# Attention and a mixture of experts on one core: sums of w2 pinned to other steps, a w1 load moved ahead, the last window in another sequence

## The chip, the cores and the metric

One Trainium2 chip, one core of it. The metric is the device time of one execution in microseconds (us). The engines are TensorE (PE in the profile), VectorE (DVE), ScalarE (ACT), GpSimd (POOL) and SyncE (SP), which here only issues DMAs. Each takes its own instructions in order.

## The reference

Attention over 4 x 8 heads of length 1152 and head size 64, where the queries are averaged in pairs; its result, reshaped, is x with 2304 tokens (N) of 512 features (D). Then a mixture of E = 8 experts with F = 1024 hidden units each, in float32:

```
logits = x @ w_gate
P = exp(logits - logits.max())
for _ in range(8):
    P /= P.sum(1, keepdims=True) + 1e-09
    P /= P.sum(0, keepdims=True) + 1e-09
    P *= N / E
for e in range(E):
    out += P[:, e:e+1] * (np.maximum(x @ w1[e], 0) @ w2[e])
```

The eight rounds are called the Sinkhorn here. Their sums over axis 0 go over all tokens, so over all partitions.

## The kernel before, in words

Every float32 product is made of three fp32r products of a high and a low part (hi x hi, lo x hi, hi x lo). "Cut" means making the two parts: hi by ScalarE (a copy to fp32r), lo by VectorE (the source less hi).

The work has three phases. The attention runs to about 371 us by a plan of its own. `moe()` (L825 to L1004) then takes the first of three groups of 768 tokens through all experts, to about 904.6 us. `late()` (L1016 on) takes groups 2 and 3, to the end at 1878.6 us.

`moe()` has 32 steps, k = (expert, quarter of F). A step makes seven products of a Strassen-like scheme for the hidden block (`product`, L886 to L894, weights of w1 stationary), combines them on VectorE (`plus`, L911), applies the relu and cuts the result (`hidden`, L900 and L901). The second products with w2 (`second`, L924; matmuls L921) are taken from a list three at a time (`some_second`) and added to x by VectorE (L937, L941). Within a step the code also prepares the next weights (class `Weights`):
- `sums1(k+1)` makes the four sums of w1's blocks that the scheme needs (L143 to L146), on VectorE for k from 2 to 8, else on GpSimd; they are the tile w1t.
- `cut1(k+1)` cuts the seven w1 blocks (w1h L157, w1l L162) and stores both parts to DRAM on SP (L170, w1c), so that `late()` need not make them again.
- `load1(k+2)` (L128) loads raw w1 (tile w1s), `cut2(k)` (L175, L176) cuts w2, `load2(k+1)` (L135) loads raw w2 into w2r or w2s in turn.
- `late()` wants four sums of each w2 block too (`sums2`, L182 to L185, on GpSimd). From step k = LATER = 5 on, `whole2(k)` makes them in place in the raw w2 tile and stores the block (w2c, L191, SP). For blocks 0 to 4 `half2` reloads one half of a block into a tile xt (L196), makes the sums and stores the half (L200); its ten calls stand in steps 10 to 19.
- The Sinkhorn on the gate matrix PR is a generator, `fill` (L855 to L880), advanced at four places of each step. Its sums over partitions are all-reduces on GpSimd: L860 (maximum) once, L875 eight times. VectorE reads their result at L862 and L876.
- In the last four steps `blocks.add` (L91 to L103) makes on GpSimd the differences of x that group 2's scheme needs.

The order of the instructions on each engine in `moe()` is made by a scheduler of the framework from what is ready. Only instructions handed to `keep_in_program_order` stay behind the ones that the code has before them on their engine: `cut2` and `blocks.add(1, ...)`. The sums and stores of w2 and the halves are not among them, and the scheduler is free to put them earlier.

`late()` is different: it hands operations with costs and priorities (`op`, smaller is earlier) to a `Plan` that lists them by engine under limits of buffers (`LATE_CAPS`), and the result stands as written. It has 64 steps (32 windows of two steps). `load_ops` (L1071) issues on SP, in order of priority: w1 of the window's first step (T - 21), the gate's row pb (T - 20), w2 (T - 16; raw parts L1087 and L1088, sums L1089), w1 of the second step (T - 7). `step_ops` makes the first products (L1064) from the stored w1 cuts; `window_ops` (L1189) makes the second products transposed (L1266): `hsum` (L1207, GpSimd) makes sums of hidden blocks hb, `cuts` the hi and lo parts of w2's and the hidden blocks (L1228 to L1243); ScalarE copies accumulators into PSUM ahead of a product where PRE or PRE_END names it (L1251), else VectorE adds the product to x (L1280). In the last window (`end`) EARLY sets how early the w2 cuts may be made and PRE_END which accumulators are fetched ahead. `join` (L1301) adds the accumulators of a group together; `finish` (L1320) transposes them (L1335), copies the result out of PSUM into tiles os, of which there are three (L1346, L1348), and stores half rows of tokens (L1353).

Of the kernel before, what the change touches and what calls it, by code (L numbers as in the profile page):

```python
# [5 lines left out]
F32 = mybir.dt.float32  # L6
# [105 lines left out]
LATER = 5  # L112


class Weights:
# [63 lines left out]
    def sums2(self, k, t):  # L179
        b11, b21, b12, b22 = t  # L180
        e = self.nc.gpsimd
        e.tensor_tensor(out=b22, in0=b12, in1=b22, op=ALU.add)  # L182
        e.tensor_tensor(out=b12, in0=b11, in1=b12, op=ALU.subtract)
        e.tensor_tensor(out=b11, in0=b22, in1=b11, op=ALU.subtract)
        e.tensor_tensor(out=b21, in0=b21, in1=b11, op=ALU.subtract)  # L185

    def whole2(self, k):
        t = self.raw2[k]
        self.sums2(k, [t[:, a, b * 2 * P:(b + 1) * 2 * P] for a in range(2) for b in range(2)])
        y = self.summed[k] = self.cuts.tile([P, 2 * D], F32, name=f"w2c{k}")  # L190
        self.nc.sync.dma_start(out=y.rearrange("p (a d) -> p a d", a=2), in_=t)  # L191

    def half2(self, k, h):
        t = self.stage.tile([P, 2, TH], F32, name="xt", tag="xt", bufs=2).rearrange("p a t -> p (a t)")[:, :4 * P].rearrange("p (a d) -> p a d", a=4)
        ds = slice(h * P, (h + 1) * P)
        self.nc.sync.dma_start(out=t, in_=self.w2[k].rearrange("p (a d) -> p a d", a=4)[:, :, ds])  # L196
        self.sums2(k, [t[:, a] for a in range(4)])
        if h == 0:
            self.summed[k] = self.cuts.tile([P, 2 * D], F32, name=f"w2c{k}")
        self.nc.sync.dma_start(out=self.summed[k].rearrange("p (a d) -> p a d", a=4)[:, :, ds], in_=t)  # L200
# [624 lines left out]
def moe(tc, out, x, ident, wg, PR, blocks, wt):  # L825
    nc = tc.nc
    with (
# [133 lines left out]

        for k in range(wt.steps):
# [15 lines left out]
            if k == 0:  # L978
                wt.cut2(0)
            wt.load1(k + 2)  # L980
            if k:
                wt.cut2(k)
            wt.load2(k + 1, "w2r" if k % 2 else "w2s")
            if k >= LATER:
                wt.whole2(k)
            if k >= wt.steps - 4:
                blocks.add(1, (3, 4, 6, 5)[k - wt.steps + 4], nc.gpsimd)
# [5 lines left out]
            if 10 <= k < 10 + 2 * LATER:  # L993
                wt.half2((k - 10) // 2, k % 2)
# [5 lines left out]
        for i in (0, 3, 4, 1, 5, 2, 6):  # L1000
            blocks.hi(1, i)
            blocks.lo(1, i)
        some_second(MT)
# [3 lines left out]
PRE, PRE_END = (0, 1, 2, 3, 4), (0, 2, 3)  # L1007
EARLY = 8
ORDER = (0, 0), (6, 2), (5, 5), (3, 3), (4, 4), (1, 1), (2, 6)
LATE_CAPS = dict(pb=2, w1=2, w2=2, hb=2, ht=1, hc=3, wc=3, e=2, mt=2, os=3)  # L1010
# [5 lines left out]
def late(tc, out, x, ident, blocks, wt):  # L1016
# [54 lines left out]
    def load_ops(j):  # L1071
        T = 28 * j
        g, e = 1 + j // PW, j % PW // 2
        if j % 2 == 0:
            @op("SP", 1600, T - 20, w=[("pb", g, e)], new=[(("pb", g, e), "pb")], lat=2500)
            def load_pb():
                y = D0["pb", g, e] = tile("pb", [TG])
# [13 lines left out]
        for s in range(2):  # L1091
            k = 2 * j + s

            @op("SP", 7000, T + 14 * s - 21, w=[("w1", k)], new=[(("w1", k), "w1")], lat=2500)
# [94 lines left out]
    def window_ops(j):  # L1189
# [10 lines left out]
        def hsum(i, a, b, r, prio):  # L1200
            new = [(HT, "ht")] if i == 5 else []

            @op("Pool", pool(2 * TH), prio, r=r, w=full({3: 3, 4: 2, 6: 1}[i]) if i != 5 else [HT], new=new, use=[HB])
# [231 lines left out]
```

## Time and profile before

| | |
|---|---|
| three executions, us | 1882.83, 1882.98, 1880.57; median 1882.83 |
| the profiled execution | 1880.4 us, of which the span from first to last instruction is 1878.6 |
| mean granted TensorE clock | 0.989 of full speed |
| busy, share of the span | TensorE 97%, VectorE 79%, ScalarE 61%, GpSimd 37% |
| the chain that ended last | TensorE 85%, VectorE 6%, GpSimd 3%, nothing the profile shows 2%, DMA 2%, ScalarE 1% |
| DMA | 366.88 MB in all, 195 GB/s mean |

Times within the profile are from the span's start. A timeline row gives start, duration, engine, line and operation, the output and input tiles, how many instructions it stands for, and in brackets how long the engine was idle before it and what released it ("issue": the engine waited for nothing that the profile shows). In the rows by stretch, busy time is given for each engine with the count of its instructions; PEclk is the mean TensorE clock that was granted, as a share of full speed. SPq is SyncE's queue of DMA issues.

### The profile page before, as it was taken

To read this page: it belongs to the slowest core of one execution; us is meant where nothing else is said; L and a number is where in the kernel's file an instruction comes from. 1 tells how busy PE (TensorE), PEld (TensorE's weight loads), DVE (VectorE), ACT (ScalarE), POOL (GpSimd) and SP (SyncE) were. 2 spreads that over 40 slices of the span, in tenths; PEclk is the share of its full clock that TensorE was granted. 3 is DMA by queue.
4 is the path that set the end of the run, shared out by engine and by line. 5 is a ranking of instruction groups with operands and counts; after the bars stand their busy time and mean duration, and the time that the engine had idled before them with its cause. 6 is when DMAs were issued, how large, how long until landed. Compare 5 with 4: busy or idle time off the path is not lost.

```text
span 1878.6 us, 32317 instructions
## 1 busy us (share of the span) xinstructions
PE 1826.6 (97%) x12324; PEld 1722.8 (92%) x12324; DVE 1481.7 (79%) x2653; ACT 1146.5 (61%) x1900; POOL 703.1 (37%) x533
## 2 busy tenths in 40 slices
PE   9999999989798999999899999999989999999997
PEld 8888888978687999998799999999989999999996
DVE  8999999788667777776468777777797878878776
ACT  7888887643223333333277677776766777777774
POOL 5555555421256434353223323233252323323224
PEclk9999999999999999999899999999999999999998
DMA  6787776386178666562754655556455565655541
GB/s 209 186 212 192 203 193 170 96 283 224 74 274 293 240 219 225 212 221 82 285 201 173 218 187 197 205 180 222 176 193 186 185 205 191 225 183 193 205 160 34
DMA packets 100279, 366.88 MB, mean 195 GB/s; under 512 B 15804, under 2 KB 39324, under 8 KB 91932
## 3 DMA queue, kind: packets, MB, share of 16 engines
q1 hardware_dynamic: 96668, 362.85, 57.6%
q8 instruction: 97, 1.59, 0.3%
q10 hardware_dynamic: 3456, 1.97, 0.3%
q14 instruction: 58, 0.48, 0.1%
HBM read 252.77 MB, written 80.34 MB: 177 GB/s over the span
## 4 chain that ended last, share of the span: by engine, by line
PE 85%; DVE 6%; POOL 3%; issue 2%; DMA 2%; ACT 1%; POOLq 0%; SPq 0%; DVEq 0%; ACTq 0%
PE mt L1266 23%; PE pso L921 10%; PE ps L566 7%; PE bA L1064 7%; PE bD L1064 7%; PE bB L1064 7%; PE ps L643 4%; PE ps L675 3%; PE bC L1064 3%; PE psh L891 3%; PE ps L689 3%; PE psh L893 3%; PE psh L892 3%; PE ps L694 1%; DVE c L911 1%
## 5 line engine op out<-in xcount | busy, mean ns | idle before, releaser
L1266 PE MATMUL mt<-hc,wc 128*128 128x384 f32 x2616 | 520.8, 335 | 5.9 <-DVE hc L1243 4.3
L1266 PEld LDWEIGHTS mt<-hc,wc 128*128 128x128 f32 x2616 | 457.7, 188 | 8.6 <-DVE hc L1243 5.9
L1207 POOL TENSOR_TENSOR hb<-hb 128x768 f32<-128x768 f32 x96 | 210.9, 2197 | 352.5 <-DVE hc L1243 347.8
L1233 DVE TENSOR_TENSOR wc<-w,wc 128x512 fp32r<-128x512 f32 x218 | 221.3, 1015 | 36.6 <-ACT wc L1228 36.6
L1243 DVE TENSOR_TENSOR hc<-hb,hc 128x768 fp32r<-128x768 f32 x192 | 190.1, 990 | 44.2 <-ACT hc L1238 44.1
L574 DVE TENSOR_SCALAR_CACHE_REDUCE E<-ps 128x384 f32<-128x384 f32 x432 | 214.9, 551 | 10.3 <-PE ps L566 9.2
L1238 ACT ACTIVATE hc<-hb 128x768 fp32r<-128x768 f32 x192 | 161.6, 842 | 51.4 <-DVE hb L1159 35.2
L1278 ACT ACTIVATE x<-mt 128x768 f32<-128x768 f32 x162 | 131.9, 814 | 99.9 <-PE mt L1266 99.5
L587 ACT ACTIVATE E<-E,st 128x1152 f32<-128x1152 f32 x144 | 179.9, 1261 | 16.8 <-DVE st L580 16.7
L1207 POOL TENSOR_TENSOR ht<-hb 128x768 f32<-128x768 f32 x32 | 60.8, 1899 | 317.0 <-DVE hb L1159 317.0
L891 PE MATMUL psh<-xch,w1h 128*128 128x384 f32 x448 | 154.3, 344 | 19.1 <-DVE u L911 5.4
L1064 PE MATMUL bA<-xch,w 128*128 128x384 f32 x512 | 151.3, 336 | 8.4 <-DMA w<-w1c 8.4
L893 PE MATMUL psh<-xch,w1l 128*128 128x384 f32 x448 | 153.3, 343 | 2.2 <-DVE w1l L162 2.2
L900 ACT ACTIVATE hh<-c 128x384 fp32r<-128x384 f32 x128 | 66.4, 522 | 145.4 <-DVE c L911 138.8
L892 PE MATMUL psh<-xcl,w1h 128*128 128x384 f32 x448 | 153.0, 341 | 0.0
L1064 PE MATMUL bD<-xch,w 128*128 128x384 f32 x512 | 151.3, 336 | 0.2 <-ACT bD L1122 0.2
L921 PE MATMUL pso<-w2h,hh 128*128 128x512 f32 x384 | 149.6, 391 | 1.8 <-DVE x L941 1.8
L1064 PE MATMUL bB<-xch,w 128*128 128x384 f32 x512 | 150.9, 335 | 0.0
L921 PE MATMUL pso<-w2l,hh 128*128 128x512 f32 x384 | 150.2, 391 | 0.0
L921 PE MATMUL pso<-w2h,hl 128*128 128x512 f32 x384 | 150.1, 391 | 0.0
L1228 ACT ACTIVATE wc<-w 128x512 fp32r<-128x512 f32 x218 | 135.9, 624 | 22.6 <-PE mt L1266 18.4
L566 PE MATMUL ps<-kT,qT 64*128 64x384 f32 (+1 forms) x1296 | 146.2, 346 | 0.1
(195 smaller groups left out, 3957.4 us busy)
## 6 DMA issues: line engine op xcount, KB each, us to landing
w<-w1c SPq DMA_DIRECT2D x64, 1792.0 KB
w<-w2c SPq DMA_DIRECT2D x64, 512.0 KB
F<-T SPq DMA_DIRECT2D x168, 184.0 KB
w1c<-w1h SPq DMA_DIRECT2D x32, 896.0 KB
w1c<-w1l SPq DMA_DIRECT2D x32, 896.0 KB
w1s<-in_moe_w_dram SPq DMA_DIRECT2D x32, 512.0 KB
w<-in_moe_w_dram SPq DMA_DIRECT2D x64, 256.0 KB
qr<-in_q_dram SPq DMA_DIRECT2D x15, 640.0 KB
```

The lines of the kernel that those rows point to most:

```text
L566: nc.tensor.matmul(ps[h][:, :PK], D["qT", p][rows, x, t * P:(t + 1) * P], D["kT", p][rows, y, j * PK:(j + 1) * PK], start=(i == 0), stop=( ...
L574: nc.vector.tensor_scalar(out=D["E", m, h][:, j * PK:(j + 1) * PK], in0=D["sc", m, j][h][:, :PK], scalar1=0.0625, scalar2=None, op0=ALU.mu ...
L587: nc.scalar.activation(out=x, in_=x, func=ACTF.Exp, bias=D["st", m][:, h, 3:4], accum_out=sums[p % RS][:, col + h * QT:col + h * QT + 1])
L891: nc.tensor.matmul(ps, hi[:, a, c, :], blocks.xch[:, b, c, :], start=(c == 0), stop=False)
L892: nc.tensor.matmul(ps, hi[:, a, c, :], blocks.xcl[:, b, c, :], start=False, stop=False)
L893: nc.tensor.matmul(ps, lo[:, a, c, :], blocks.xch[:, b, c, :], start=False, stop=(c == 1))
L921: nc.tensor.matmul(ps, u[:, fh, ms], w, start=(n == 0), stop=(n == 11))
L1064: nc.tensor.matmul(o, w, v, start=start, stop=stop, skip_group_check=True)
L1207: nc.gpsimd.tensor_tensor(out=hblock(i), in0=D0[HB][:, a], in1=D0[HB][:, b], op=sub)
L1233: nc.vector.tensor_tensor(out=y[:, 1], in0=wsrc(), in1=y[:, 0].bitcast(F32), op=sub)
L1243: nc.vector.tensor_tensor(out=y[:, 1], in0=hblock(b), in1=y[:, 0].bitcast(F32), op=sub)
L1266: nc.tensor.matmul(o, w[:, y, s, ds], v[:, z, s], start=(i == 0 and not pre), stop=(i == 5), skip_group_check=pre)
```

## The change

It touches four places.
- w2's sums: LATER is 9, so blocks 0 to 8 are reloaded in halves (18 instead of 10), and whole blocks are summed from k = 9. A half is now a job of three stages: load in step 9 + n, sums a step later, store a step after that. All sums, loads and stores of it, the sums of whole blocks, and their stores are pinned in program order. The store of block k - 1 stands in step k between the w1 load and the w2 load, and the last two are issued on ScalarE's queue after the cuts of group 2's x.
- The additions for group 2 at the last four steps stand ahead of the loads.
- `late()`: the first pb tile is allocated first, and w1 of the second step is loaded right behind w1 of the first.
- The end: EARLY, PRE_END, the last window's sums hsum on VectorE and ahead, its cuts in another sequence, and four tiles xs in place of os for the output's first three token tiles.

```diff
@@ -109,7 +109,7 @@
         self.nc.vector.tensor_tensor(out=self.xcl[:, i], in0=self.src(g, i), in1=self.xch[:, i].bitcast(F32), op=ALU.subtract)
-LATER = 5
+LATER = 9
 class Weights:
@@ -176,28 +176,32 @@
         self.tc.keep_in_program_order(self.nc.vector.tensor_tensor(out=lo, in0=self.raw2[k], in1=hi.bitcast(F32), op=ALU.subtract))
         self.b[k] = (hi, lo)
-    def sums2(self, k, t):
+    def sums2(self, t):
         b11, b21, b12, b22 = t
-        e = self.nc.gpsimd
-        e.tensor_tensor(out=b22, in0=b12, in1=b22, op=ALU.add)
-        e.tensor_tensor(out=b12, in0=b11, in1=b12, op=ALU.subtract)
-        e.tensor_tensor(out=b11, in0=b22, in1=b11, op=ALU.subtract)
-        e.tensor_tensor(out=b21, in0=b21, in1=b11, op=ALU.subtract)
+        e, pin = self.nc.gpsimd, self.tc.keep_in_program_order
+        pin(e.tensor_tensor(out=b22, in0=b12, in1=b22, op=ALU.add))
+        pin(e.tensor_tensor(out=b12, in0=b11, in1=b12, op=ALU.subtract))
+        pin(e.tensor_tensor(out=b11, in0=b22, in1=b11, op=ALU.subtract))
+        pin(e.tensor_tensor(out=b21, in0=b21, in1=b11, op=ALU.subtract))
     def whole2(self, k):
         t = self.raw2[k]
-        self.sums2(k, [t[:, a, b * 2 * P:(b + 1) * 2 * P] for a in range(2) for b in range(2)])
+        self.sums2([t[:, a, b * 2 * P:(b + 1) * 2 * P] for a in range(2) for b in range(2)])
+
+    def store2(self, k, q):
         y = self.summed[k] = self.cuts.tile([P, 2 * D], F32, name=f"w2c{k}")
-        self.nc.sync.dma_start(out=y.rearrange("p (a d) -> p a d", a=2), in_=t)
+        self.tc.keep_in_program_order(q.dma_start(out=y.rearrange("p (a d) -> p a d", a=2), in_=self.raw2[k]))
     def half2(self, k, h):
         t = self.stage.tile([P, 2, TH], F32, name="xt", tag="xt", bufs=2).rearrange("p a t -> p (a t)")[:, :4 * P].rearrange("p (a d) -> p a d", a=4)
         ds = slice(h * P, (h + 1) * P)
-        self.nc.sync.dma_start(out=t, in_=self.w2[k].rearrange("p (a d) -> p a d", a=4)[:, :, ds])
-        self.sums2(k, [t[:, a] for a in range(4)])
+        self.tc.keep_in_program_order(self.nc.sync.dma_start(out=t, in_=self.w2[k].rearrange("p (a d) -> p a d", a=4)[:, :, ds]))
+        yield
+        self.sums2([t[:, a] for a in range(4)])
         if h == 0:
             self.summed[k] = self.cuts.tile([P, 2 * D], F32, name=f"w2c{k}")
-        self.nc.sync.dma_start(out=self.summed[k].rearrange("p (a d) -> p a d", a=4)[:, :, ds], in_=t)
+        yield
+        self.tc.keep_in_program_order(self.nc.sync.dma_start(out=self.summed[k].rearrange("p (a d) -> p a d", a=4)[:, :, ds], in_=t))
 class Plan:
@@ -959,6 +963,7 @@
                 if todo:
                     second(*todo.pop(0))
+        jobs = []
         for k in range(wt.steps):
             hids[k] = [hid.tile([P, 2, TG], F32R, name=nm, tag=nm) for nm in ("hh", "hl")]
             p1 = keep(product(k, 0, 0), "p1")
@@ -977,21 +982,25 @@
             wt.cut1(k + 1)
             if k == 0:
                 wt.cut2(0)
+            if k >= wt.steps - 4:
+                blocks.add(1, (3, 4, 6, 5)[k - wt.steps + 4], nc.gpsimd)
             wt.load1(k + 2)
             if k:
                 wt.cut2(k)
+            if LATER < k < wt.steps - 1:
+                wt.store2(k - 1, nc.sync)
             wt.load2(k + 1, "w2r" if k % 2 else "w2s")
             if k >= LATER:
                 wt.whole2(k)
-            if k >= wt.steps - 4:
-                blocks.add(1, (3, 4, 6, 5)[k - wt.steps + 4], nc.gpsimd)
+            if 9 <= k < 9 + 2 * LATER:
+                jobs.append(wt.half2((k - 9) // 2, (k - 9) % 2))
+            for y in jobs:
+                next(y, None)
             if k == 0:
                 last_gate()
                 fill = sinkhorn()
             if k == 2 * FQ:
                 spread()
-            if 10 <= k < 10 + 2 * LATER:
-                wt.half2((k - 10) // 2, k % 2)
             some_second(3)
             next(fill, None)
             next(fill, None)
@@ -1000,14 +1009,16 @@
         for i in (0, 3, 4, 1, 5, 2, 6):
             blocks.hi(1, i)
             blocks.lo(1, i)
+        for k in (wt.steps - 2, wt.steps - 1):
+            wt.store2(k, nc.scalar)
         some_second(MT)
 SLOT = 1040
-PRE, PRE_END = (0, 1, 2, 3, 4), (0, 2, 3)
-EARLY = 8
+PRE, PRE_END = (0, 1, 2, 3, 4), (0, 1, 3, 4)
+EARLY = 12
 ORDER = (0, 0), (6, 2), (5, 5), (3, 3), (4, 4), (1, 1), (2, 6)
-LATE_CAPS = dict(pb=2, w1=2, w2=2, hb=2, ht=1, hc=3, wc=3, e=2, mt=2, os=3)
+LATE_CAPS = dict(pb=2, w1=2, w2=2, xs=4, hb=2, ht=1, hc=3, wc=3, e=2, mt=2, os=3)
 OUT = {(0, 0): 1, (0, 1): 6, (1, 0): 2, (1, 1): 3}
@@ -1074,7 +1085,7 @@
         if j % 2 == 0:
             @op("SP", 1600, T - 20, w=[("pb", g, e)], new=[(("pb", g, e), "pb")], lat=2500)
             def load_pb():
-                y = D0["pb", g, e] = tile("pb", [TG])
+                y = D0["pb", g, e] = tile("pb", [TG]) if j else first_pb
                 n = (g - 1) * MT
                 nc.sync.dma_start(out=y, in_=wt.spread[e, n:n + MT].rearrange("n t -> (n t)").unsqueeze(0).to_broadcast([P, TG]))
@@ -1091,7 +1102,7 @@
         for s in range(2):
             k = 2 * j + s
-            @op("SP", 7000, T + 14 * s - 21, w=[("w1", k)], new=[(("w1", k), "w1")], lat=2500)
+            @op("SP", 7000, T + 14 * s - (21 if k != 1 else 34.5), w=[("w1", k)], new=[(("w1", k), "w1")], lat=2500)
             def load_w1(k=k):
                 y = D0["w1", k] = tile("w1", [2, 7, 2, P], F32R)
                 nc.sync.dma_start(out=y.bitcast(F32), in_=wt.kept[k % (E * FQ)])
@@ -1200,11 +1211,11 @@
         def hsum(i, a, b, r, prio):
             new = [(HT, "ht")] if i == 5 else []
-            @op("Pool", pool(2 * TH), prio, r=r, w=full({3: 3, 4: 2, 6: 1}[i]) if i != 5 else [HT], new=new, use=[HB])
+            @op("DVE" if end else "Pool", dve(2 * TH) if end else pool(2 * TH), prio, r=r, w=full({3: 3, 4: 2, 6: 1}[i]) if i != 5 else [HT], new=new, use=[HB])
             def hsums():
                 if new:
                     D0[HT] = tile("ht", [2, TH])
-                nc.gpsimd.tensor_tensor(out=hblock(i), in0=D0[HB][:, a], in1=D0[HB][:, b], op=sub)
+                (nc.vector if end else nc.gpsimd).tensor_tensor(out=hblock(i), in0=D0[HB][:, a], in1=D0[HB][:, b], op=sub)
         def cuts(n, a, b):
             slot = T + 4 * n + 1
@@ -1279,19 +1290,33 @@
                     else:
                         nc.vector.tensor_tensor(out=y, in0=t, in1=y, op=ALU.add)
-        cuts(0, *ORDER[0])
-        cuts(1, *ORDER[1])
-        hsum(5, 2, 3, full(2) + full(3), T - 1)
-        cuts(2, *ORDER[2])
-        hsum(3, 3, 0, full(3) + full(0), T + 1)
-        cuts(3, *ORDER[3])
-        hsum(4, 2, 3, full(2) + full(3), T + 5)
-        cuts(4, *ORDER[4])
-        if j % PW == PW - 1:
+        if end:
+            cuts(0, *ORDER[0])
+            cuts(1, *ORDER[1])
+            hsum(5, 2, 3, full(2) + full(3), T - 1)
+            hsum(3, 3, 0, full(3) + full(0), T)
+            hsum(4, 2, 3, full(2) + full(3), T + 1)
+            cuts(2, *ORDER[4])
+            cuts(3, *ORDER[2])
+            cuts(4, *ORDER[3])
             join(g)
-        cuts(5, *ORDER[5])
-        hsum(6, 1, 2, full(1) + full(2), T + 14)
-        cuts(6, *ORDER[6])
+            cuts(5, *ORDER[5])
+            hsum(6, 1, 2, full(1) + full(2), T + 14)
+            cuts(6, *ORDER[6])
+        else:
+            cuts(0, *ORDER[0])
+            cuts(1, *ORDER[1])
+            hsum(5, 2, 3, full(2) + full(3), T - 1)
+            cuts(2, *ORDER[2])
+            hsum(3, 3, 0, full(3) + full(0), T + 1)
+            cuts(3, *ORDER[3])
+            hsum(4, 2, 3, full(2) + full(3), T + 5)
+            cuts(4, *ORDER[4])
+            if j % PW == PW - 1:
+                join(g)
+            cuts(5, *ORDER[5])
+            hsum(6, 1, 2, full(1) + full(2), T + 14)
+            cuts(6, *ORDER[6])
         if end:
             finish(g)
@@ -1316,6 +1341,9 @@
         both(4, 4, 3, T + 5)
         both(3, 5, 3, T + 6)
         both(6, 4, 6, T + 7)
+
+    def late_tile():
+        return sb.tile([P, 2, TH], F32, name="xs", tag="xs", bufs=4).rearrange("p a t -> p (a t)")[:, :D]
     def finish(g):
         T = 28 * PW * g + 27
@@ -1334,13 +1362,13 @@
                     for db in range(2):
                         nc.tensor.transpose(y[:, (2 * dh + db) * P:(2 * dh + db + 1) * P], acc(g, OUT[dh, th])[:, db, ts], ident)
-                nos = [] if dh else [(OS, "os")]
+                nos = [] if dh else [(OS, "os" if i > 2 else "xs")]
                 @op(("ACT", "DVE"), [act(256), dve(256)], pr + dh * (1.5 if th else 3) + 0.5, r=[("t", g, i, dh), own[i]] + ([("o", g, i, 0)] if dh else []),
                     w=[("o", g, i, dh)], new=nos, use=[OS] if dh else [])
                 def put(eng, i=i, dh=dh, OT=OT, OS=OS):
                     if dh == 0:
-                        D0[OS] = tile("os", [D])
+                        D0[OS] = tile("os", [D]) if i > 2 else late_tile()
                     y, z = (t[:, dh * 256:dh * 256 + 256] for t in (D0[OS], D0[OT]))
                     if eng == "ACT":
                         nc.scalar.activation(out=y, in_=z, func=ACTF.Copy)
@@ -1371,6 +1399,7 @@
             def x_lo(i=i):
                 blocks.lo(g, i)
+    first_pb = tile("pb", [TG])
     seed("B")
     seed("C")
     for g in range(1, G):
```

## Rows read from the trace of the kernel before

**Rows 1.** Busy time by stretch: each engine's us (instructions), then PEclk, DMA share, GB/s.

```profile
371.00:420.00 49.00, 43.52 (x235) 39.12 (x233) 40.18 (x89) 22.18 (x40) 15.13 (x25) 0.97 0.78 275
480.00:499.00 19.00, 13.81 (x68) 12.87 (x67) 10.46 (x27) 2.89 (x6) 1.15 (x2) 0.91 0.23 96
499.00:523.00 24.00, 18.18 (x74) 15.24 (x73) 15.64 (x27) 4.00 (x8) 11.89 (x16) 0.86 0.37 124
523.00:580.20 57.20, 50.84 (x247) 44.12 (x245) 41.30 (x59) 20.28 (x32) 35.82 (x44) 0.98 0.72 261
580.20:600.00 19.80, 19.80 (x91) 18.36 (x92) 16.24 (x25) 6.42 (x11) 9.51 (x13) 0.89 0.88 313
600.00:880.00 280.00, 280.00 (x1411) 254.01 (x1410) 207.78 (x323) 96.52 (x163) 116.10 (x147) 1.00 0.59 212
912.40:920.80 8.40, 0.00 (x0) 0.00 (x0) 2.90 (x5) 1.15 (x2) 0.00 (x0) 0.70 0.79 300
920.80:927.00 6.20, 6.16 (x22) 6.19 (x23) 0.00 (x0) 1.37 (x3) 0.00 (x0) 0.58 0.99 392
1837.50:1865.00 27.50, 22.65 (x118) 21.29 (x116) 23.05 (x22) 13.45 (x19) 13.44 (x7) 0.94 0.00 1
1865.00:1878.60 13.60, 4.92 (x24) 3.56 (x22) 4.52 (x9) 2.58 (x7) 4.67 (x2) 0.74 0.35 116
```

**Rows 2.** Timeline of TensorE, two stops.

```profile
485.91 0.69 PE L891 MATMUL psh<-xch,w1h 128*128 128x384 f32 x1 [5.19 <-DVE u L911]
...
515.98 0.45 PE L891 MATMUL psh<-xch,w1h 128*128 128x384 f32 x1 [3.41 <-ACT w1h L157]
```

**Rows 3.** Timeline of GpSimd, 396 to 515 us.

```profile
396.03 0.43 POOL L875 PARTITION_ALL_REDUCE ca<-cs  x1 [5.27 <-DVE cs L872]
...
484.56 0.43 POOL L875 PARTITION_ALL_REDUCE ca<-cs  x1 [7.24 <-issue]
...
492.47 0.73 POOL L183 TENSOR_TENSOR w2s<-w2s 128x256 f32<-128x256 f32 x1 [7.48 <-issue]
...
506.62 0.73 POOL L184 TENSOR_TENSOR w2s<-w2s 128x256 f32<-128x256 f32 x1 [7.01 <-issue]
...
514.12 0.71 POOL L146 TENSOR_TENSOR w1t<-w1s,w1t 128x256 f32<-128x256 f32 x1
```

**Rows 4.** Timeline of VectorE, its read of an all-reduce.

```profile
485.02 0.17 DVE L876 TENSOR_SCALAR ca<-ca 128x8 f32<-128x8 f32 x1 [6.15 <-POOL ca L875]
```

**Rows 5.** Timeline of GpSimd, first and last sum of two halves.

```profile
603.20 0.89 POOL L182 TENSOR_TENSOR xt<-xt 128x128 f32<-128x128 f32 x1
...
608.41 0.47 POOL L185 TENSOR_TENSOR xt<-xt 128x128 f32<-128x128 f32 x1
```

**Rows 6.** Timeline of SyncE's queue, two loads of w1.

```profile
593.34 0.84 SPq L128 DMA_DIRECT2D w1s<-in_moe_w_dram  x1
...
606.95 0.41 SPq L128 DMA_DIRECT2D w1s<-in_moe_w_dram  x1
```

**Rows 7.** Timeline of ScalarE, the same copy in two steps.

```profile
858.57 0.49 ACT L906 ACTIVATE p<-psh 128x384 f32<-128x384 f32 x1 [1.42 <-PE psh L893]
...
874.08 0.49 ACT L906 ACTIVATE p<-psh 128x384 f32<-128x384 f32 x1 [8.21 <-PE psh L893]
```

**Rows 8.** Waits of SyncE's queue: us in total, times, longest us.

```profile
SPq L135 <- DMA w2c<-w2s: 26.1, 9, 4.7
```

**Rows 9.** Timeline of SyncE's queue, from the first group to the late part.

```profile
893.14 0.32 SPq L1079 DMA_DIRECT2D pb<-spread  x1
...
913.48 0.80 SPq L1097 DMA_DIRECT2D w<-w1c  x2
```

**Rows 10.** Timeline of VectorE in the last window.

```profile
1838.78 2.35 DVE L1243 TENSOR_TENSOR hc<-hb,hc 128x768 fp32r<-128x768 f32 x1
...
1843.32 0.94 DVE L1243 TENSOR_TENSOR hc<-hb,hc 128x768 fp32r<-128x768 f32 x1
```

**Rows 11.** Timeline of ScalarE in the output's last copies.

```profile
1872.87 0.38 ACT L1346 ACTIVATE os<-bC 128x256 f32<-128x256 f32 x1 [1.53 <-DMA out_dram<-os]
```

## The prediction

> **What bounds the kernel now.** The busy time by stretch comes first [rows 1]. From 600 to 880 us TensorE is busy 280.00 of 280.00 us at full clock, so the first token group's steps need nothing but TensorE there. Between 371 and 600 us the same loop leaves it idle, and each stop is followed by a stretch at part clock (0.89 means that some of it ran at the lower of the two levels, 1.2 instead of 2.4 GHz). I count a stop as idle time plus (1 - granted clock) x stretch, where the stretch is nearly all busy or its idle part ran at full clock:
> - A, 371 to 420: 49.00 - 43.52 = 5.5 idle, 0.03 x 49 = 1.5: 7.0 us
> - B, 480 to 499: 5.2 idle, 0.09 x 19 = 1.7: 6.9 us
> - C, 499 to 523: 5.8 idle, 0.14 x 24 = 3.4: 9.2 us
> - D, 523 to 600: 6.4 idle, 0.11 x 19.8 = 2.2: 8.6 us
>
> Together 31.7 us. What ends the stops is read from TensorE's timeline [rows 2]: at 485.91 it had waited 5.19 us for VectorE, at 515.98 3.41 us for ScalarE's cut of w1. Behind both stands GpSimd [rows 3]. An all-reduce of the Sinkhorn gate starts at 396.03, right after its input, and takes 0.43 us. But where sums of w2 (L182 to L185) come between, each change costs about 7 us in which nothing that the profile shows is waited for: 7.24 before the all-reduce at 484.56, 7.48 before the sum at 492.47, 7.01 before the one at 506.62. VectorE works in order and stands for 6.15 us at its read of the all-reduce [rows 4], with TensorE's inputs behind it: that is B. When the all-reduces are over, the held-up sums run as one block from 506.62, and the sums of w1 end in it at 514.83 (514.12 + 0.71), just ahead of TensorE's wait for the cut: that is C. A and D have the same shape, a block of w2 sums ahead of w1's.
>
> **The change, part by part.** The profiled execution took 1880.4 us (span 1878.6), 2.4 below the median of 1882.83. All sums are against 1880.4.
>
> *Sums and stores of w2 (LATER 9, half2 as three pinned steps, whole2 pinned, store2 a step later).* In steps 0 to 8 GpSimd loses all w2 sums; w1's sums for steps 2 to 8 are VectorE's already. With nothing between the all-reduces the changes go, except one into the first and one out of the last. The Sinkhorn takes two to three points of `fill` per step and should be over by step 5, some 80 us after 372. So A, B and C go: 7.0 + 6.9 + 9.2 = 23.1 us. D is half counted, 4.3: its block of delayed sums is gone, but the new halves start at step 9, in the same stretch. Sum 27.4; bounds 13 (A and C only in part) and 31.7.
> Against it: four more blocks come back in halves. Two halves take from 603.20 to 608.88 [rows 5], 2.84 us each; one per step in steps 9 to 26, of which 10 are made now, earlier, so 8 x 2.84 = 23 us are new, less the 16 whole-block sums of k = 5 to 8, 16 x 0.73 = 12 (0.73 at 492.47) [rows 3]. GpSimd is busy 116.10 of 280 [rows 1], so they fit. SP gets eight loads and a net four stores more, and each is pinned; the order per step is w1c stores, w1 load, w2c store, w2 load, half load, half store. From the w1 load at 593.34 to the next at 606.95 is 13.61 us [rows 6] with one step of TensorE at 15.51 (874.08 - 858.57) [rows 7]. So the loop that feeds TensorE has 1.9 us to spare, and the SP part lies beside the w1 load's flight and the sums. Taken at nothing; if that cover is gone the price is in the rivals. The two last stores on ACT's queue stand before the output stores (L943) and behind the hi cuts of the next group; their sums are long made, and ACT has no work that TensorE needs there. Nothing. The additions for group 1 at steps 28 to 31 only move ahead in the same step on an engine with room: nothing.
>
> One page speaks to the added GpSimd work. The rows show VectorE's two-input operations longer beside a GpSimd sum: 2.35 us at 1838.78 against 0.94 alone [rows 10]. The Trainium skill, page "SBUF — State Buffer", section "Who interferes with whom", says that such an instruction with both inputs in SBUF contends with a GpSimd instruction that reads SBUF; the trace agrees (2.35 against 0.94). By it every new half could stop VectorE for up to its 2.84 us. VectorE is busy 207.78 of 280 [rows 1], 11.5 per step; with 2.84 it is 14.3 of 15.5. It fits, by little; this feeds the first rival's chance.
>
> *w1(1) loaded right behind w1(0).* In the late part's first step TensorE is done at 912.4 and idle for 8.40 us, then runs 6.20 us at clock 0.58 [rows 1]: 8.4 + 0.42 x 6.2 = 11.0. It waited for w1(1), issued only at 913.48 behind the first w2 loads, which wait for the old products, while SP had nothing from 893.14 on [rows 9]. Behind w1(0) it goes out ten or more us earlier and has 20 us to land; it takes about 7 (913.48 to 920.8 now, beside others). w1(2), issued at about the same time as now, is due one step later and is perhaps 1 us short: 10 us gained. Bounds 2 (it still waits for its buffer) and 11.
>
> *Group boundary.* EARLY, PRE_END and the end's order are the last window's only, but a planner places all: 0, with 3 either way.
>
> *The end.* In 1837.5 to 1865 TensorE loses 27.5 - 22.65 = 4.9 idle and 0.06 x 27.5 = 1.6 clock [rows 1], 6.5 us, with VectorE busy 23.05 of it. Four sums move from GpSimd to VectorE at about 0.95 each, 3.8 us more; three operations there lose their stretching by a sum (2.35 against 0.94, 1.4 each) [rows 10], 4.2 less; one accumulator more fetched ahead by ScalarE saves a 0.94 addition. VectorE gains about 1.5, and the sums come first: I take 2.5 of 6.5. In the tail ScalarE waits 1.53 us for an output buffer [rows 11]; with four more buffers that goes: 1.5. Sum 4; bounds 9 and -2.
>
> Sum: 27.4 + 10 + 0 + 4 = 41.4, so 1880.4 - 41.4 = **1839.0**. Its own range is 1828 to 1850 (49 of gain with all stops gone and 3 of the boundary; 30 with D kept, the boundary at -3 and the end at 0).
>
> **Rivals.**
> 1. *The feeding loop becomes the bound in steps 9 to 26.* If the half (2.84) falls ahead of w1's sums in GpSimd's order, 13.61 + 2.84 = 16.45 exceeds 15.51 by 0.94; x 18 steps is 17 us: 1839 + 17 = 1856. For it: stops A and D are just this. Against: two halves at 603.20 cost nothing [rows 1, 5]. 0.15.
> 2. *w1(1) still comes late* because its buffer or a finished DMA holds it: 8 to 10 of the gain stay out, 1848. For it: SP waits there for many things. 0.08.
> 3. *Slower: the pinned SP order itself closes the loop.* A w2 load waits for the landing of the w2c store in its buffer, 26.1 us in 9 times = 2.9 each now [rows 8], and a half's load for the store two halves earlier, another 2.9. If both lie in series with the next w1 load, 13.61 + 5.8 = 19.4 against 15.51 is 3.9 x 18 = 70 us: 1839 + 70 = 1909. It decides as soon as over 1.9 us of the 5.8 is in series. Against: they are queued behind the w1 load, beside that load's own flight and the sums of w1. 0.06.
> 4. *The change doesn't do what it says:* the 7 us belong to the all-reduce and not to the change of operation, and B stays: 1839 + 7 = 1846. Against: 396.03, an all-reduce that follows an all-reduce at once [rows 3]. 0.05.
> 5. *The stops come again at other steps* and nothing is gained beyond a few us: 1878 to 1882. 0.03.
>
> **How the numbers follow.** The forecast has 0.63, and its time is the prediction. Rivals 1, 2 and 4 lie within 1856, rivals 3 and 5 beyond. The range 1826 to 1858 leaves out those two (0.09) and some of each tail. A measurement can tell about 0.2%, 3.8 us, from no change: faster 0.91, within 0.03, slower 0.06.
>
> **What would show it.** Right: GpSimd's all-reduces 0.1 us behind their inputs in one unbroken run, no gap of 7 us but the first and last; TensorE without idle from about 390 to the late part; one step at 15.5 throughout; w1(1) issued before 900 and the step at 912 without a stop; the late part shifted by about 37 us with its own length shorter by the end's 4. Wrong: steps of 16 us or more between 520 and 800 with TensorE waiting for the cut of w1 (rivals 1 and 3, told apart by whether GpSimd or SP stands), TensorE waiting for w1c at the second late step (2), or all-reduces still 7 us behind their inputs (4).

## The result, and the profile after

The changed kernel takes 1836.49 us (median; 1834.25 to 1838.17), the kernel before 1881.7 us beside it; the ratio is 0.9761, with a 95% interval of 0.9744 to 0.9777. The forecast was 1839.0. The profiled executions are 1880.4 us with a span of 1878.6 before, and 1834.25 with 1832.5 after: the span is 46.1 us shorter. The lines moved a little: in the changed kernel the all-reduces are L879, the w1 loads of the late part L1108, its first products L1075 and L1080, its second products L1277, the sums `hsum` L1218, the joins L1335.

Busy time by stretch of the changed kernel, columns as in [rows 1]:

```profile
371.00:420.00 49.00, 48.11 (x254) 42.83 (x253) 46.18 (x118) 23.94 (x43) 7.07 (x11) 1.00 0.62 226
420.00:523.00 103.00, 103.00 (x523) 93.81 (x522) 89.90 (x178) 40.55 (x69) 21.46 (x31) 1.00 0.64 230
523.00:600.00 77.00, 77.00 (x389) 69.89 (x388) 60.39 (x91) 27.03 (x45) 42.88 (x61) 1.00 0.69 246
600.00:830.00 230.00, 230.00 (x1160) 208.65 (x1159) 183.13 (x267) 79.38 (x131) 128.91 (x169) 1.00 0.71 252
1320.00:1375.00 55.00, 49.98 (x284) 48.76 (x283) 50.50 (x53) 33.75 (x53) 27.33 (x12) 1.00 0.46 161
```

Where stops A to D were, TensorE is now busy in all but 0.9 us, at full clock; in this profile the first group runs without another wait until the late part. The stretch around 1350, the boundary of groups 2 and 3, is another matter: 5.0 us idle there, as in the kernel before, where the boundary lies 43 us later:

```profile
1355.00:1420.00 65.00, 59.98 (x341) 58.76 (x341) 58.47 (x62) 41.93 (x67) 29.49 (x14) 1.00 0.49 180
```

GpSimd's timeline of the changed kernel: the first two and the last of the nine all-reduces, and the first sum behind them:

```profile
385.31 0.38 POOL L864 PARTITION_ALL_REDUCE gmxa<-gmx  x1 [7.68 <-DVE gmx L861]
...
389.77 0.43 POOL L879 PARTITION_ALL_REDUCE ca<-cs  x1 [4.08 <-DVE cs L876]
...
440.08 0.40 POOL L879 PARTITION_ALL_REDUCE ca<-cs  x1 [8.13 <-DVE cs L876]
...
472.80 0.74 POOL L143 TENSOR_TENSOR w1t<-w1s 128x256 f32<-128x256 f32 x1 [32.32 <-DMA w1s<-in_moe_w_dram]
```

This answers to [rows 3]. The eight all-reduces of L879 follow each other with no other instruction between, each released by its input cs and none by "issue". The sum of w1 behind the last one comes 32 us later, when its load has landed; whatever the change of operation costs there is hidden.

The queue of GpSimd has one more sign of the changes of operation: a pair of MODIFY_POOL_CONFIG records at each. Two of the lines that carry them in the kernel before (times, their durations in ns, first and last start in us), and then all of them in the changed one:

```profile
L875 POOLq MODIFY_POOL_CONFIG  x12: 1/4/11, 407.3 to 493.4; - x12
L182 POOLq MODIFY_POOL_CONFIG  x6: 88/108/108, 396.4 to 468.7; - x6
```

```profile
L864 POOLq MODIFY_POOL_CONFIG  x2: 8/8/8, 377.6 to 377.6; - x2
L143 POOLq MODIFY_POOL_CONFIG  x2: 88/88/88, 440.4 to 440.5; - x2
```

In the kernel before there are 28 records (the others are 2 at L860, 4 at L183 and 4 at L184), so 14 changes between 382 and 500 us; in the changed one there are 4, one change into the run of all-reduces and one out of it.

SyncE's queue of the changed kernel where [rows 9] showed the w1 load behind the w2 loads:

```profile
846.37 12.38 SPq L1108 DMA_DIRECT2D w<-w1c  x2
...
858.43 0.32 SPq L1108 DMA_DIRECT2D w<-w1c  x1
...
867.03 0.32 SPq L1090 DMA_DIRECT2D pb<-spread  x1
```

The first row merges two loads; the next shows the second of them by itself. Both w1 loads of the first late steps now go out, at 846.37 and 858.43, ahead of pb, and TensorE has no stop at the second late step (the idle time from 870.8 to 900 is 0.9 us in all).

Three points that both programs have in common split the 46.1 us: the first instruction of the late part on TensorE, and two waits at the boundary of groups 2 and 3. TensorE's timeline of the kernel before, then of the changed one:

```profile
904.58 0.33 PE L1069 MATMUL bB<-xch 128*128 128x384 f32 x1
...
1376.09 2.18 PE L1266 MATMUL mt<-hc,wc 128*128 128x384 f32 x11 [1.70 <-DVE hc L1243]
...
1408.34 1.17 PE L1266 MATMUL mt<-hc,wc 128*128 128x384 f32 x5 [1.18 <-DVE hc L1243]
```

```profile
870.87 0.33 PE L1080 MATMUL bB<-xch 128*128 128x384 f32 x1
...
1332.64 2.20 PE L1277 MATMUL mt<-hc,wc 128*128 128x384 f32 x11 [1.70 <-DVE hc L1254]
...
1364.91 1.16 PE L1277 MATMUL mt<-hc,wc 128*128 128x384 f32 x5 [1.18 <-DVE hc L1254]
```

So 904.58 - 870.87 = 33.7 us were gained by the end of the first group; 1376.09 - 1332.64 = 43.45, so 9.7 more at the transition; 43.43 at 1364.91, so nothing in the boundary; and 46.1 at the end, so 2.7 in the last window and the tail. Of the 33.7, 1.05 us lie ahead of the group: its first product starts at 372.29 before and at 371.24 after. From there to the late part the group lasts 532.3 and 499.6 us, 32.7 less. This is itself uncertain: in the ten profiles with this first group, which differ only in `late()` (the experiments below), it lasts 499.6 to 503.4 us, so by the one profile of the kernel before the first group's gain is 28.9 to 32.7 us.

### The profile page after: what moved, and what is told of

Read it like the earlier page. It is cut to its first block, busy times and chain, and to the rows that moved or that the text cites. A ratio compares the mean times of both kernels' runs of the same rounds, so it can differ in the third digit from the quotient of the medians.

```text
span 1832.5 us, 32306 instructions
## 1 busy us (share of the span) xinstructions
PE 1813.3 (99%) x12324; PEld 1712.2 (93%) x12324; DVE 1495.9 (82%) x2656; ACT 1149.0 (63%) x1902; POOL 696.5 (38%) x545
## 4 chain that ended last, share of the span: by engine, by line
PE 74%; DVE 3%; ACT 1%; DMA 1%; issue 0%; POOL 0%; SPq 0%; POOLq 0%; DVEq 0%; ACTq 0%
PE mt L1277 24%; PE pso L925 14%; PE bB L1075 7%; PE bD L1075 7%; PE bA L1075 7%; PE psh L897 4%; PE psh L895 4%; PE psh L896 4%; PE bC L1075 3%; DVE hc L1254 1%; DVE wc L1244 1%; DMA w<-w2c 0%; DVE x L1335 0%; DMA out_dram<-x 0%; DVE x L1291 0%
## 5 line engine op out<-in xcount | busy, mean ns | idle before, releaser
L1277 PE MATMUL mt<-hc,wc 128*128 128x384 f32 x2616 | 521.9, 336 | 7.2 <-DVE hc L1254 5.5
L1277 PEld LDWEIGHTS mt<-hc,wc 128*128 128x128 f32 x2616 | 458.9, 188 | 10.3 <-DVE hc L1254 6.9
L1218 POOL TENSOR_TENSOR hb<-hb 128x768 f32<-128x768 f32 x93 | 204.4, 2198 | 344.5 <-DVE hc L1254 339.9
L1218 POOL TENSOR_TENSOR ht<-hb 128x768 f32<-128x768 f32 x31 | 58.9, 1901 | 306.3 <-DVE hb L1170 306.3
L1075 PE MATMUL bB<-xch,w 128*128 128x384 f32 x512 | 150.6, 334 | 0.5 <-ACT bB L1133 0.5
L1075 PE MATMUL bD<-xch,w 128*128 128x384 f32 x512 | 150.6, 334 | 0.2 <-ACT bD L1133 0.2
L1075 PE MATMUL bA<-xch,w 128*128 128x384 f32 x512 | 150.5, 334 | 0.0
L895 PE MATMUL psh<-xch,w1h 128*128 128x384 f32 x448 | 150.2, 335 | 0.0
```

The lines of the kernel that those rows point to most:

```text
L895: nc.tensor.matmul(ps, hi[:, a, c, :], blocks.xch[:, b, c, :], start=(c == 0), stop=False)
L1075: nc.tensor.matmul(o, w, v, start=start, stop=stop, skip_group_check=True)
L1218: (nc.vector if end else nc.gpsimd).tensor_tensor(out=hblock(i), in0=D0[HB][:, a], in1=D0[HB][:, b], op=sub)
L1277: nc.tensor.matmul(o, w[:, y, s, ds], v[:, z, s], start=(i == 0 and not pre), stop=(i == 5), skip_group_check=pre)
```

## The experiments

Each kernel is the changed one with the edit shown (`...` marks code left out). They were measured in groups, with the kernel before beside each group: its median was 1881.7 us beside the changed kernel, 1878.7 beside e1, e2 and e4, 1883.0 beside e5 to e8, 1880.4 beside c1 to c4 and 1879.1 beside d1. So kernels of different groups are compared by the ratio to it as well as by the median. "The late part" is from TensorE's first instruction in it to the end of the span. Three parts of the change were not run by themselves: the additions ahead of the loads, the two stores on ScalarE's queue, and the first pb tile.

### The pin, the place, and the price of a change of operation

**e1: the pins taken away, the later steps kept.**

```diff
-        e, pin = self.nc.gpsimd, self.tc.keep_in_program_order
+        e, pin = self.nc.gpsimd, lambda y: y
...
-        self.tc.keep_in_program_order(q.dma_start(out=y..., in_=self.raw2[k]))
+        q.dma_start(out=y..., in_=self.raw2[k])
```

(the load and the store of a half alike)

> The kernel after, with the w2 sums, half loads and stores no longer pinned; LATER stays 9 and the halves are still called from step 9 on. Theory (the order on GpSimd decides, and only the pin keeps it): the half sums slip back between the all-reduces, gaps of about 7 us return at most of them, stops A and B of the kernel before come back (7.0 + 6.9 us) and part of C; 14 to 22 us over the changed kernel, 1850 to 1859 us. Rival (the later step of the calls is enough): within 4 us of the changed kernel's 1836.5.

Measured: 1872.4 us, ratio to before 0.9965 (0.9953 to 0.9976). That is far worse than my 1850 to 1859. GpSimd's timeline in this kernel:

```profile
396.28 0.43 POOL L879 PARTITION_ALL_REDUCE ca<-cs  x1 [5.74 <-DVE cs L876]
...
403.64 0.88 POOL L182 TENSOR_TENSOR xt<-xt 128x128 f32<-128x128 f32 x2 [6.92 <-issue]
...
413.93 0.43 POOL L879 PARTITION_ALL_REDUCE ca<-cs  x1 [6.50 <-issue]
...
421.38 0.45 POOL L182 TENSOR_TENSOR xt<-xt 128x128 f32<-128x128 f32 x1 [7.02 <-issue]
```

The scheduler takes the half sums up again between the all-reduces, though the code calls them from step 9 on, and the gaps of about 7 us are back in both directions. The busy time by stretch:

```profile
371.00:420.00 49.00, 42.39 (x220) 38.03 (x215) 38.32 (x86) 20.66 (x37) 14.78 (x24) 0.93 0.72 252
480.00:523.00 43.00, 32.49 (x150) 28.08 (x150) 27.52 (x55) 9.82 (x19) 13.09 (x18) 0.88 0.21 79
600.00:700.00 100.00, 93.11 (x450) 84.15 (x449) 74.68 (x112) 34.22 (x58) 53.64 (x69) 0.95 0.69 242
```

A is back and a little larger (6.6 us idle and clock 0.93), the stretch from 480 to 523 loses 10.5 us idle, about what B and C did, and 6.9 us idle come up anew between 600 and 700, in three waits of 2.1 to 2.5 us. My range had only part of C in it and nothing behind it. The late part begins at 907.60, 3 us later than in the kernel before. What e1 still gains against before is in the late part, which lasts 963.0 us (1870.6 - 907.60) where it took 974.0 (1878.6 - 904.58). So for the first group the later place alone gave nothing; the pins decide. e1 takes the pins of the sums and those of the loads and stores away together, and does not tell them apart. Why TensorE stops between 600 and 700 was not followed.

**e2: LATER = 5, pins kept.**

```diff
-LATER = 9
+LATER = 5
```

> The kernel after with LATER = 5, all pins kept: blocks 5 to 8 are summed whole again, eight halves fewer. Theory (only sums that fall between the all-reduces cost; those end at 440.5 us in the changed kernel, and step 5 begins at about 450): no difference beyond 2 us, 1834.5 to 1838.5 us, and TensorE again without idle time in the first group's steps. Rival (the move from step 5 to step 9 was needed, by GpSimd's backlog as in stops C and D): 9 to 18 us more, 1845 to 1854 us.

Measured: 1838.2 us, ratio 0.9784 (0.977 to 0.9799). The median lies within the 2 us named; by the ratio it is 4 us above the changed kernel, with overlapping intervals, so the two are not told apart. TensorE waits 1.1 us in all from 420 to 480 and not at all from 480 to 871. So moving the sums of four more blocks out of steps 5 to 8 was not what the kernel needed; the Sinkhorn ends at 440.5, before step 5. With e1 this comes close to a test of the pins alone: nearly the old places, with pins, keep the gain, and the new places without pins lose it.

**e5: one small addition in each Sinkhorn round.**

```diff
-                nc.gpsimd.partition_all_reduce(ca, cs, ...)
+                cm = gs.tile([P, E], F32, name="cm", tag="cm")
+                nc.gpsimd.tensor_tensor(out=cm, in0=cs, in1=cs, op=ALU.add)
+                nc.gpsimd.partition_all_reduce(ca, cm, ...)
...
-... scalar1=float(N / E)
+... scalar1=float(2 * N / E)
```

> The kernel after with one more GpSimd instruction in each of the eight Sinkhorn rounds: an addition of the 128x8 tile cs to itself, whose result the all-reduce takes (the factor behind it is doubled to match). Theory (each change between an all-reduce and a tensor_tensor costs about 7 us, however little the instruction does): from cs to ca some 14 us pass instead of 0.5, the eight rounds last 120 to 180 us instead of 55, VectorE stands at each read, TensorE loses 40 to 100 us: 1877 to 1937 us. Rivals (the 7 us are the all-reduce's own; or it was the amount of work that held things up, and eight such additions are under 3 us): within 4 us of 1836.5.

Measured: 1865.74 us, ratio 0.9915 (0.9894 to 0.9935), 29 us over the changed kernel. GpSimd's timeline:

```profile
441.94 0.19 POOL L880 TENSOR_TENSOR cm<-cs 128x8 f32<-128x8 f32 x1 [7.31 <-DVE x L943]
...
450.11 0.43 POOL L881 PARTITION_ALL_REDUCE ca<-cm  x1 [7.98 <-issue]
...
457.97 0.21 POOL L880 TENSOR_TENSOR cm<-cs 128x8 f32<-128x8 f32 x1 [7.44 <-DVE w1l L162]
```

and what waited for the all-reduces, in us, times, and the longest:

```profile
POOL ca L881 <- issue: 57.2, 8, 8.5
...
DVE ca L882 <- POOL ca L881: 29.3, 8, 12.2
```

An addition that takes 0.19 us, seldom more (up to 1.06), makes the all-reduce behind it 5.9 to 8.5 us late: 57.2 us in eight rounds, 7.15 each (in the last round a sum of w1 lies between them too). Seven of the additions themselves start 7.0 to 7.9 us after GpSimd's last work. The engine named in the bracket is not what they wait for: their input cs had been ready for 1.1 to 4.0 us (before 441.94 it ends at 440.82). From the first all-reduce to the last 125 us pass instead of 55, and GpSimd's queue has 36 MODIFY_POOL_CONFIG records instead of 4. So the price hangs on the change of operation, not on the work done. My range for the loss was too high because VectorE stands for half of it only, 29.3 us, about what the time grew by. The Trainium skill, page "GPSIMD Engine Reference", section "2.1 Instruction dispatch", states that the first call to a freshly loaded kernel of GpSimd costs about 6 us that no instruction in the profile shows. The trace is near it, with 7.15 us on the way to the all-reduce and 7.0 to 7.9 us on the way back; that each change is such a first call, no run here shows.

### The w1 load

**e4: the old priority.**

```diff
-            @op("SP", 7000, T + 14 * s - (21 if k != 1 else 34.5), ...
+            @op("SP", 7000, T + 14 * s - 21, ...
```

> The kernel after with the late part's second w1 load at its old priority, behind pb and w2. Theory (the early load took the stop at the second late step away): the stop of 8.4 us waiting for w1c and the half-clock stretch return, 9 to 11 us more, 1845.5 to 1847.5 us. Rival (the load comes in time either way once the stores of the w2 sums are out of SP's way): within 2 us of 1836.5.

Measured: 1846.05 us, ratio 0.9825 (0.981 to 0.9839), 9.6 us over the changed kernel. The late part is 9.1 us longer by the profiles, 970.8 us (1842.2 - 871.44) against 961.6 (1832.5 - 870.87). TensorE's timeline has the old stop back, first in the kernel before, then in e4:

```profile
920.84 0.66 PE L1064 MATMUL bA<-xch,w 128*128 128x384 f32 x1 [8.44 <-DMA w<-w1c]
```

```profile
887.78 0.66 PE L1075 MATMUL bA<-xch,w 128*128 128x384 f32 x1 [8.53 <-DMA w<-w1c]
```

### The end

**e6 and c2: the whole last part undone**, measured twice; c1 is the changed kernel itself, measured beside c2.

```diff
-PRE, PRE_END = (0, 1, 2, 3, 4), (0, 1, 3, 4)
-EARLY = 12
+PRE, PRE_END = (0, 1, 2, 3, 4), (0, 2, 3)
+EARLY = 8
...
-        if end:
+        if False:
             cuts(0, *ORDER[0])
```

(with the sums on GpSimd as in e7 and the output tiles as in e8)

> The kernel after with the whole last part of the change undone: sums of the last window on GpSimd in the old sequence, EARLY 8, PRE_END (0, 2, 3), all output tiles in os. Theory (from the same points of both traces, the part after the group boundary gave 2.7 of the 46 us): 2 to 4 us more, 1838.5 to 1840.5 us. Rival (the prediction's 4 us): 1840 to 1842. Rival (nothing, the 2.7 us came from elsewhere): within 1 us of 1836.5.

> The changed kernel itself again, so that the versions of this call are compared with it on one chip. Every theory: its ratio to the kernel before within 0.2% of 0.976.

> The kernel after with the whole last part undone once more, now beside the changed kernel on one chip. Theory (the last part is worth 2 to 4 us): 2 to 4 us above the changed kernel of this call. Rival (nothing): within 1 us of it.

Measured: e6 1839.18 us (ratio 0.9775, 0.9761 to 0.979); c1 1836.27 (0.9767, 0.9753 to 0.9782); c2 1838.17 (0.978, 0.9764 to 0.9795). Undone it is 2.7 and 1.9 us longer by the medians, at the low end of what was expected, and the intervals of the ratios overlap. By the profiles the late part lasts 961.6 us in c1 (1834.5 - 872.92), 965.6 in c2 (1837.5 - 871.88) and 966.9 in e6 (1840.6 - 873.71): 4.0 and 5.3 more. e2, whose late part has the same code as c1's, lasts 963.6 there, so single profiles differ by 2 us. The end is worth 2 to 5 us, and no closer than that; that it is worth anything rests on all these differences having one sign.

**e7: the four sums back on GpSimd; e8: all output tiles in os.**

```diff
-            @op("DVE" if end else "Pool", dve(2 * TH) if end else pool(2 * TH), prio, ...
+            @op("Pool", pool(2 * TH), prio, ...
...
```

```diff
...
-                        D0[OS] = tile("os", [D]) if i > 2 else late_tile()
+                        D0[OS] = tile("os", [D])
```

> The kernel after, only the last window's four sums back on GpSimd, in the new sequence. Theory (a GpSimd sum stretches the VectorE operations beside it from 0.94 to 2.35 us, which is worse than 0.95 us for the sum itself): 1 to 3 us more, 1837.5 to 1839.5 us. Rival (VectorE is the bound, four sums more on it cost what they save): within 1 us, or up to 2 us less, 1834.5 to 1837.5.

> The kernel after, only the output's first three token tiles back in os (three buffers) instead of xs. Theory (the tail from the last second product is 12.5 us against 13.6 before, and the wait of 1.53 us for a buffer is what went): 1 to 1.5 us more, 1837.5 to 1838 us. Rival (stores of the output follow each other on SP anyway, so the buffers hide nothing): within 0.4 us of 1836.5.

Measured: e7 1837.9 us (0.9768, 0.9754 to 0.9782), e8 1837.66 (0.9766, 0.9751 to 0.9781). Both are 1.2 to 1.4 us above the changed kernel's median and neither is told apart from it, so which piece of the end is worth what stays open.

### A better version

VectorE's timeline at the end of the changed kernel shows what the change left:

```profile
1813.38 2.49 DVE L1218 TENSOR_TENSOR hb<-hb 128x768 f32<-128x768 f32 x1
...
1817.66 2.60 DVE L1335 TENSOR_TENSOR x<-x 128x768 f32<-128x768 f32 x1
```

These are a sum and a join that take 0.95 us each alone, stretched to 2.5 and 2.6 beside joins that GpSimd still makes (from 1812.54 to 1815.05 and from 1816.81 to 1819.44). And at the boundary of groups 2 and 3:

```profile
1330.00 2.58 DVE L1254 TENSOR_TENSOR hc<-hb,hc 128x768 fp32r<-128x768 f32 x1
...
1333.37 2.32 DVE L1244 TENSOR_TENSOR wc<-w,wc 128x512 fp32r<-128x512 f32 x1
```

**c3: the last joins on VectorE, three late stores from ScalarE's queue; c4: the boundary's sums on VectorE; d1: both.**

```diff
-            @op(("DVE", "Pool"), [dve(2 * TH), pool(2 * TH)], prio, ...
+            @op(*((("DVE", "Pool"), [dve(2 * TH), pool(2 * TH)]) if g == 1 else (("DVE",), [dve(2 * TH)])), prio, ...
...
+                tail = g > 1 and dh == 1 and i < 3
-                @op("SP", 400, ...
+                @op("ACT" if tail else "SP", 100 if tail else 400, ...
...
```

```diff
+            by_dve = end or j in (PW - 1, PW)
-            @op("DVE" if end else "Pool", dve(2 * TH) if end else pool(2 * TH), prio, ...
+            @op("DVE" if by_dve else "Pool", dve(2 * TH) if by_dve else pool(2 * TH), prio, ...
...
```

> The kernel after, with two edits at its end: the last group's joins of accumulators all on VectorE (0.95 us each, none on GpSimd, whose adds of 1.8 to 2.6 us stretch VectorE's beside them to 1.9 to 2.6), and the second halves of the last three output tiles stored from ScalarE's queue instead of SyncE's, which was still issuing 2 us after the last copy. Theory (stretching and the one queue of stores set the tail): 1.5 to 3 us less than the changed kernel of this call. Rival (VectorE's work at the end is the bound, four more additions cost what they save): within 1 us of it.

> The kernel after, with the eight sums of the two windows at the boundary of groups 2 and 3 on VectorE instead of GpSimd, as the change did at the end. Theory (the 5 us that TensorE is idle there come from VectorE operations stretched beside GpSimd's sums): 1 to 4 us less than the changed kernel of this call. Rival (VectorE is full there, 50.5 of 55 us, and eight sums more make it the bound): 2 to 6 us more.

> The kernel after with both edits together: the boundary windows' sums on VectorE, the last group's joins on VectorE and three of the last stores from ScalarE's queue. Theory (the two places are 470 us apart and share nothing, so 3.0 and 5.0 us add up): 1827 to 1830 us, ratio to the kernel before 0.971 to 0.974. Rival (the new order of the plan at one place costs at the other): no better than 1831.3, the boundary edit alone.

Measured: c3 1833.31 us (0.975, 0.9736 to 0.9763), c4 1831.31 (0.9741, 0.9728 to 0.9754), d1 1829.01 (0.9733, 0.9717 to 0.9749). c3 and c4 are 3.0 and 5.0 us under c1, measured beside them; c3's interval overlaps c1's and c4's just touches it. d1's lies below c1's, and its slowest execution (1830.15) is faster than the fastest of the changed kernel (1834.25). So d1 beats the changed kernel, by 5 to 6 us by the ratios and 7 by the medians. Its interval overlaps c4's, so by the times the rival (no better than c4) is not refuted. In c4 the stretch of the boundary reads

```profile
1320.00:1375.00 55.00, 53.13 (x296) 52.49 (x296) 50.49 (x62) 34.95 (x57) 16.07 (x5) 0.97 0.48 172
```

TensorE's idle time there fell from 5.0 to 1.9 us, though at a clock of 0.97, with VectorE as busy as before (50.49 against 50.50 us): it makes seven of the eight sums within this stretch, in the time that the stretching took. The profiles place the gains. From the start of the late part to VectorE's operation L1146 behind the boundary (1374.07 in the changed kernel, 1371.86 in c4) 503.2 us pass in the changed kernel and in c1, 500.3 in c4 and 498.8 in d1; from there to the end 458.4 in c1, 455.0 in c3 and 454.4 in d1. So by the profiles the boundary edit is worth 2.9 to 4.4 us and the edit at the end 3.4 to 4.0, and in d1 they add up. c4's 5.0 us by the medians is more than its profile accounts for: 1.4 of the 3.8 us between the spans of c1 and c4 arise in the first group, where both have the same code.

## Why the prediction was right

- *Stops A to D: mechanism right, the term too small.* 32.7 us against 27.4 (28.9 to 32.7 over the ten profiles). The half that I held back was D: the step "D is half counted ... but the new halves start at step 9, in the same stretch" failed. TensorE is busy 77.00 of 77 us there with a half in nearly every step. All four together were counted at 31.7, which lies within the 28.9 to 32.7; the clock of D's first stretch, 0.02 x 57.20 = 1.1 us, was not in it. e5 shows the cause that I named, the change of operation, and the 14 changes of before against 2 bear it out; e1 shows that the pins, not the place, took it away.
- *"Taken at nothing": nearly right, and closer than it looked.* GpSimd's order is exactly what the first rival feared: the sums of two halves, from 517.79 and from 531.42 on, stand ahead of w1's sums at 520.14 and 533.67. In this profile the loop held, as TensorE is busy throughout. SyncE's queue, first and last load of w1 in the loaded steps:

```profile
526.85 0.84 SPq L128 DMA_DIRECT2D w1s<-in_moe_w_dram  x1
...
806.17 0.37 SPq L128 DMA_DIRECT2D w1s<-in_moe_w_dram  x1
```

That is 279.3 us for 18 steps, 15.52 each, TensorE's pace of 15.51. The 13.61 us on which the 1.9 us to spare rest were one interval and no bound of the loop: here single intervals go from 14.2 to 16.8. In four of the ten profiles the loop does stop TensorE between 720 and 800 us, by 0.6 us (c1), 1.4 (c3), 1.7 (e6) and 2.7 (e8). The two waits of e8:

```profile
722.42 0.45 PE L895 MATMUL psh<-xch,w1h 128*128 128x384 f32 x1 [1.53 <-DVE c L915]
...
755.31 0.44 PE L895 MATMUL psh<-xch,w1h 128*128 128x384 f32 x1 [1.20 <-DVE c L915]
```

- *Rival 3, the SP order: its waits came, and hardly decided.* The waits on SyncE's queue, in us, times, longest:

```profile
SPq L135 <- DMA w2c<-w2s: 70.6, 11, 7.9
...
SPq L198 <- DMA w2c<-xt: 55.0, 16, 3.9
```

A w2 load waits 6.4 us for the store (70.6 / 11) where it was 2.9 in [rows 8], a half load 3.4 (55.0 / 16): 9.8 against the 5.8 that I priced. On SyncE's queue they stand between one w1 load and the next, but beside the w1 load's flight, the sums and the cuts, as the prediction had it. Added to the 13.61 us they would have been far more than the 1.9 us that TensorE's step leaves. They leave almost no slack, though: in e8 a w1 load goes out 16.81 us after the one before (687.24 and 704.05), behind a w2 load that waited 7.1 us, its data keeps ScalarE's cut at 712.59 waiting for 3.28 us, and the first of the two waits above follows. That looks like rival 3 on a small scale; no run isolates it.
- *The page on the ports of SBUF:* the sentence that halves might stop VectorE and still fit came out so: in the changed kernel's profile no stop is left in the loaded steps. At the end and the boundary the stretching does decide: the same 128x768 operation takes 0.95 us alone and 2.5 to 2.6 beside a GpSimd addition, and with the sums off GpSimd TensorE's idle time at the boundary fell by 3.1 us in c4. The Trainium skill, page "SBUF — State Buffer", section "Who interferes with whom", has it that a VectorE instruction with both inputs in SBUF contends with a GpSimd instruction that reads SBUF; the trace agrees (0.95 against 2.5 to 2.6).
- *The transition:* 9.7 us against 10, and 9.1 to 9.6 by e4. Rival 2 fell, but its cause was there: the second w1 load stood for 11.6 us behind the landing of a w2c store, and still went out at 858.43, 12 us ahead of the late part.
- *Boundary:* 0 against 0.
- *The end:* 2.7 us against 4 by the profile, 2 to 5 by e6 and c2: the sign held, the size is not known closer, and e7 and e8 don't tell its two pieces apart. One thing was left out of VectorE's side: I priced the four sums at 0.95 each, but the joins stay on GpSimd, and one sum beside them takes 2.49.
- *Rivals 4 and 5:* both fell. Without a change of operation an all-reduce waits for nothing but its input.

By the profiles 46.1 us were gained against the 41.4 of the sum. The 4.7 between them are 6.3 too little up to the late part (5.3 in the first group, and 1.05 ahead of it that no term was for), less 1.3 and 0.3 at the end and the transition. The lower bound of the sum's own range does not follow from its terms: a gain of 49 gives 1831.4 us, not 1828; the measured 1836.49 lies inside either way. That the median came within 2.5 us of the forecast is in part luck: the execution profiled after lay 2.2 us under its median, and from profile to profile the sum was 4.7 short.

## What to carry to other kernels

A cheap instruction on a shared engine can be dear by what it stands between: look in the timeline for idle time that nothing releases ("issue"), and see whether the kind of operation changes there; then group the kinds and pin the group, since an order that only the source has is not an order. Where two engines slow each other down, moving the slower one's small operations to the faster one can be free even when that one looks full, for part of its busy time may be the stretching itself, as in c4.

## What was not expected

Calling the sums later without the pin moved them nowhere: the scheduler put them between the all-reduces again, and the first group ended 3 us later than in the kernel before (907.60 against 904.58). An addition of 0.19 us cost about 7 us on each side of it. And VectorE took over the sums of the boundary, seven of them in this stretch, with its busy time unchanged (50.50 and 50.49 us of 55), while TensorE's idle time fell by 3.1 us.
